# A fused attention and MLP layer: query blocks outermost, exponentials of 1536 columns, gelu once per block

## The chip, the cores and the metric

One core of one Trainium2 chip. All times are device microseconds (us) of one execution. The profile lists five engines: TensorE (PE; PEld is its weight load), ScalarE (ACT), VectorE (DVE), GpSimd (POOL) and SyncE (SP), which issues most of the DMAs on the pages here. The kernel before takes 1041.75 us (median of 3 runs, 1039.78 to 1043.16).

## The reference, cut to what matters

Sequence 2048, model width 512, 32 heads of 16, hidden width 1792, everything bf16:

```python
xn  = layernorm(x)
qkv = xn @ wqkv                               # 32 heads, Dh = 16
p   = softmax(q @ k.T * Dh ** -0.5)           # 32 x 2048 x 2048 exponentials
a   = (p @ v) @ wo
h   = gelu(layernorm(xn) @ w1 + b1)           # tanh form of gelu
out = x + a + h @ w2 + b2
```

The 134 million exponentials decide: in calls of 128 partitions (128x1024 before, mostly 128x1536 after) they are 1,048,576 columns, and both kernels compute all of them on ScalarE. Scores lie transposed (128 keys by 512 queries per head), so one *unit* of work is 512 columns; there are 2048 units.

## The kernel before

The outer loop goes over 8 sets of four heads, inside it over 4 query blocks of 512 and 16 key tiles. Per key tile: one *gang* of four small score matmuls, one for each head, on 32 rows of the array each (the four together last 0.40 us at 467.57, one such matmul 0.39 on average); two exponentials of two units; and one gang of four small p x v matmuls, which accumulate into one bank, o.

```python
psc = pctx.enter_context(tc.tile_pool(name="psc", bufs=3, space=PSUM))   # scores: three of two banks
...
for r in range(NR):                       # s, qt, kt
    emit_act(2 * r)                       # exp, 1024 columns
    if r + 1 < NR:
        emit_qk(r + 1)                    # 4 score matmuls
    if r >= 1:
        emit_pv(r - 1)                    # 4 p x v matmuls
    done = jobs.run(dense_per_round)      # up to 2.4 full matmuls of other work
    ...                                   # fills (zeros times ones) up to pe_fill = 3.0
    emit_act(2 * r + 1)
```

Three more places matter. The norms take square roots on ScalarE and go through all 16 token tiles before the first score. The MLP computes gelu from tanh, one call and four VectorE passes for each of 56 hidden tiles. Its results, and those of the output projection, are added to an f32 accumulator on VectorE:

```python
nc.scalar.activation(out=sd1[:], in_=mv[:, :, 1], func=AF.Sqrt, bias=eps_t[:], scale=1.0)
...
nc.vector.scalar_tensor_tensor(out=u[:, fi, :], in0=pre[:, fi, :], scalar=0.044715, ...)
nc.vector.scalar_tensor_tensor(out=u[:, fi, :], in0=u[:, fi, :], scalar=1.0, ...)
nc.scalar.activation(out=uv, in_=uv, func=AF.Tanh, scale=GELU_C)
nc.vector.scalar_tensor_tensor(out=ht[:, f0 + fi, :], in0=u[:, fi, :], scalar=1.0, ...)
...
groups = [[0, 1, 2], [3, 4, 5], list(range(6, NS - 1)), [NS - 1]]   # output projection, in pieces
```

Of the kernel before, what the change touches and what calls it, by code (L numbers as in the profile page):

```python
# [26 lines left out]
BOUND_INFL = 0.505  # L27
L_MIN = 1e-25
L_MAX = 1e6
GELU_C = float(np.sqrt(2.0 / np.pi))  # L30
_DBG = os.environ.get("PSM_DBG")


class _Jobs:

    NPRIO = 4

    def __init__(self, held):
        self.q = [[] for _ in range(self.NPRIO)]
        self.credit = 0.0  # L40
        self.held = held
        self.sticky = None
        self.activity = 0.0
        self.paused = set()

    def add(self, gen, prio):
        self.q[prio].append(gen)
        return gen

    def _first(self):  # L50
        if self.sticky is not None:
            return self.sticky
        for q in self.q:
            if q and q[0] not in self.paused:
                return q
        return None

    def step(self):
        q = self._first()
        if q is None:  # L60
            return None
        g = q[0]
        try:
            c = next(g)
        except StopIteration:
            q.pop(0)
            c = 0
            assert not self.held(), "job finished while holding the misc bank"
        self.sticky = q if self.held() else None
        if c == "pause":  # L70
            assert self.sticky is None
            self.paused.add(g)
            c = 0
        if isinstance(c, tuple):
            c, a = c
        else:
            a = c
        self.activity += a
        return c

    def run(self, budget):
        self.credit = min(self.credit, 0.0) + budget
        self.activity = 0.0
        self.paused = set()
        while self.credit > 0.0:
            c = self.step()
            if c is None:
                break
            self.credit -= c
        return self.activity  # L90

    def pending(self, gen):
        return any(gen in q for q in self.q)

    def finish(self, gen):
        while self.pending(gen):
            self.paused = set()
            self.step()

    def drain(self):  # L100
        while True:
            self.paused = set()
            if self.step() is None:
                break
        self.credit = 0.0
# [3 lines left out]
def kernel(  # L109
# [11 lines left out]
    dense_per_round: float = 2.4,  # L121
    pe_fill: float = 3.0,
# [13 lines left out]
    NKT = S // P  # L136
    TQ = QW // P
    assert S % QW == 0 and D % P == 0 and F % P == 0 and H % HS == 0
    SW = HS * DH
    NCH = QW // 32  # L140

    const = ctx.enter_context(tc.tile_pool(name="const", bufs=1))
    big = ctx.enter_context(tc.tile_pool(name="big", bufs=1))

    def gate_on(mm, gate):
        if gate is not None:
            tc.add_manual_dep(mm.ins, gate.ins.name, ORDER_DEP, reason="order gate")

# [3 lines left out]
    seln = const.tile([P, P], BF, name="seln")  # L152
    selr = const.tile([P, P], BF, name="selr")
    eps_t = const.tile([P, 1], F32, name="eps_t")
    onescol = const.tile([P, 1], F32, name="onescol")
    onescol2 = const.tile([P, 1], F32, name="onescol2")
    okmin = const.tile([P, 1], F32, name="okmin")
    ones_f = const.tile([P, 1], F32, name="ones_f")
    r2m1 = const.tile([P, NT], F32, name="r2m1")
    b1_sb = const.tile([P, FC], BF, name="b1_sb")  # L160
    b2_sb = const.tile([1, D], BF, name="b2_sb")
    flag_i = const.tile([1, 1], I32, name="flag_i")
    wq_pad = big.tile([P, JC, H, 32], BF, name="wq_pad")
    wk_pad = big.tile([P, JC, H, 32], BF, name="wk_pad")
    wv_sb = big.tile([P, JC, D], BF, name="wv_sb")
    wo_pad = big.tile([P, NS, D], BF, name="wo_pad")
    w1_sb = big.tile([P, JC, F], BF, name="w1_sb")
    w2_sb = big.tile([P, FC, D], BF, name="w2_sb")
    va_bufs = [big.tile([P, NKT, HS, 32], BF, name=f"va{i}") for i in range(2)]
    acc = big.tile([P, NT, D], F32, name="acc")  # L170
    kt0p = big.tile([P, S], BF, name="kt0p")
    kmx0 = const.tile([P, NQT], F32, name="kmx0")
    xnT_c = [big.tile([P, JC, QW], BF, name=f"xnT{tq}") for tq in range(NQT)]
    r2m1b = big.tile([P, S], BF, name="r2m1b")
# [3 lines left out]
    G = 4  # L178

    def load_acc(gate=None):  # L180
        for t0_ in range(0, NT, G):
            d_ = nc.gpsimd.dma_start(acc[:, t0_:t0_ + G, :], xv[:, t0_:t0_ + G, :])
            if gate is not None:
                tc.add_manual_dep(d_.ins, gate.ins.name, SYNC_DEP, reason="x first")

    with tc.tile_pool(name="start", bufs=1) as st, \
            tc.tile_pool(name="startw", bufs=3) as stw, \
            tc.tile_pool(name="pst", bufs=3, space=PSUM) as pst, \
            tc.tile_pool(name="psk", bufs=4, space=PSUM) as psk, \
            tc.tile_pool(name="psw", bufs=1, space=PSUM) as psw:  # L190
        x_sb = st.tile([P, NT, D], BF, name="x_sb")
        for gi_, t0_ in enumerate(range(0, NT, G)):
            (nc.sync if gi_ % 2 == 0 else nc.scalar).dma_start(
                x_sb[:, t0_:t0_ + G, :], xv[:, t0_:t0_ + G, :])
        with nc.allow_non_contiguous_dma(reason="tiny bias load"):
            nc.scalar.dma_start(b1_sb[:], B_b1.rearrange("(fc p) -> p fc", p=P))
        nc.scalar.dma_start(b2_sb[:], B_b2[None, :])

        make_identity(nc, ident_bf[:])
        nc.vector.memset(ones_bf[:], 1.0)  # L200
        nc.vector.memset(zeros_bf[:], 0.0)
        nc.vector.memset(ones_f[:], 1.0)
        nc.vector.memset(seln[:], 0.0)
        nc.vector.memset(selr[:], 0.0)
        for j in range(HS):
            nc.vector.memset(seln[32 * j:32 * j + DH, 32 * j + DH:32 * j + DH + 1], 1.0)
            nc.vector.memset(selr[32 * j:32 * j + 1, 32 * j + DH:32 * j + DH + 2], 1.0)
        nc.vector.memset(eps_t[:], LN_EPS)
        nc.vector.memset(okmin[:], 1.0)
        pm0 = psw.tile([P, 1], F32, tag="w", name="pm0")  # L210
        nc.tensor.matmul(pm0[:], lhsT=selr[:], rhs=ones_bf[:, 0:1], start=True, stop=True)
        nc.vector.tensor_copy(onescol2[:], pm0[:])
        for j in range(HS):
            nc.vector.memset(selr[32 * j:32 * j + 1, 32 * j + DH + 1:32 * j + DH + 2], 0.0)
        pm1 = psw.tile([P, 1], F32, tag="w", name="pm1")
        nc.tensor.matmul(pm1[:], lhsT=selr[:], rhs=ones_bf[:, 0:1], start=True, stop=True)
        nc.vector.tensor_copy(onescol[:], pm1[:])
        for jc in range(JC):
            nc.vector.memset(wk_pad[:, jc, :, DH:32], 0.0)
            nc.gpsimd.memset(wq_pad[:, jc, :, DH:32], 0.0)  # L220
        for va_i in va_bufs:
            nc.gpsimd.memset(va_i[:].rearrange("p k j r -> p (k j r)"), 0.0)
            nc.gpsimd.memset(va_i[:, :, :, DH:DH + 1], 1.0)

        stats = st.tile([P, NT, nc.vector.BN_STATS_DIM], F32, name="stats")
        mv = st.tile([P, NT, nc.vector.BN_AGGR_DIM], F32, name="mv")
        sd1 = st.tile([P, NT], F32, name="sd1")
        sd2 = st.tile([P, NT], F32, name="sd2")
        r1 = st.tile([P, NT], F32, name="r1")
        v2 = st.tile([P, NT], F32, name="v2")  # L230
        assert D <= nc.vector.BN_STATS_FMAX
        gate_stat = None
        for t in range(NT):
            nc.vector.bn_stats(out=stats[:, t, :], in_=x_sb[:, t, :])  # L234
            ag = nc.vector.bn_aggr(out=mv[:, t, :], in_=stats[:, t, :])
            if t == min(NT - 1, 2 * G):
                gate_stat = ag
        wqk = st.tile([P, JC, 2 * D], BF, name="wqk")
        wo_v = A_wo.rearrange("(s j r) c -> j r s c", j=HS, r=DH)
        loads = [(wqk[:, :, D:2 * D], wv_view[:, :, D:2 * D]),  # L240
                 (wqk[:, :, 0:D], wv_view[:, :, 0:D]),
                 (wv_sb[:], wv_view[:, :, 2 * D:3 * D]),
                 (w1_sb[:], B_w1.rearrange("(jc p) f -> p jc f", p=P)),
                 (w2_sb[:], B_w2.rearrange("(fc p) d -> p fc d", p=P))]
# [56 lines left out]
    def run_pass(slow):  # L301
# [43 lines left out]
        class _Ring:  # L345
# [5 lines left out]
            @staticmethod  # L351
            def first(mm):
                return mm
# [531 lines left out]
```

## Time and profile before

To compare the two kernels I use one account for both. For each exponential I take from the trace the time from its start to the start of the next one. Unhindered this is 0.903 us for 1024 columns in the kernel before and 1.330 for 1536 in the changed one. The 0.427 between them for 512 columns are 0.834 ns a column, which leaves 0.05 us a call; the sums below use columns x 0.8333 ns + 50 ns, which gives both. Their sum is the *floor*; what a step takes beyond it is other ScalarE work or a stall.

| kernel before, us of its profiled run (span 1038.8) | |
|---|---|
| first exponential starts | 40.2 |
| floor of 1024 exponentials | 925.0 |
| 56 tanh calls at 0.52 | 29.1 |
| stalls of ScalarE (rest of 60.4 beyond the floor) | 31.3 |
| from the last exponential's end to the span's end | 12.9 |

(The prediction used 0.91 for a step, so it has 932 for this floor and 25 for these stalls.) Next, the view of waits, with its columns: who waited, for whom; us in total, how often, longest.

```profile
ACT p L751 <- PE sc L741: 13.2, 31, 2.2
```

Exponentials waited visibly for score matmuls only 31 times, never over 2.2 us. The kernel before is close to its floor everywhere but at the start.

### The profile page before, as it was taken

How to read it: one execution, taken by the hardware profiler on the slowest of the kernel's cores; microseconds unless marked ns; L12 is line 12 of the kernel's file. 1: busy time of each engine (PE TensorE's matmuls, PEld its weight loads, DVE VectorE, ACT ScalarE, POOL GpSimd, SP SyncE). 2: the span in 40 equal slices, each digit the busy share in tenths (PEclk: the TensorE clock that was granted, in tenths of full speed). 3: DMA queues.
4: the chain of work that ended last, by engine and by line, in shares of the span. 5: the costliest groups of instructions: out<-in, count | busy, mean ns of one | idle time of the engine just before them, and what ended most of it. 6: DMA issues, size and time to landing. Idle time of an engine off the chain costs nothing.

```text
span 1038.8 us, 15620 instructions
## 1 busy us (share of the span) xinstructions
PE 835.0 (80%) x6085; PEld 251.2 (24%) x6197; DVE 452.5 (44%) x976; ACT 988.0 (95%) x1106; POOL 13.2 (1%) x19
## 2 busy tenths in 40 slices
PE   5778877888778889888778887788888877788885
PEld 2312221222212222222222222122222222222221
DVE  8543894513954413536924259451134432112222
ACT  2799999999999999999999999999999999999995
POOL 5000000000000000000000000000000000000000
PEclk8999999999989999999999999999999999999998
DMA  8800000000000000000000000000000000000000
GB/s 256 210 1 1 2 1 1 1 1 1 1 1 1 2 1 1 1 2 1 1 1 1 2 1 1 1 2 1 1 2 1 1 1 1 1 1 21 21 22 23
DMA packets 12913, 15.22 MB, mean 15 GB/s; under 512 B 2337, under 2 KB 10274, under 8 KB 12834
## 3 DMA queue, kind: packets, MB, share of 16 engines
q1 hardware_dynamic: 6704, 7.87, 2.9%
q0 software_dynamic: 2112, 4.19, 1.2%
q10 hardware_dynamic: 4018, 2.10, 0.7%
q8 instruction: 50, 0.82, 0.3%
q14 instruction: 29, 0.24, 0.1%
HBM read 9.97 MB, written 2.10 MB: 12 GB/s over the span
## 4 chain that ended last, share of the span: by engine, by line
ACT 56%; PE 22%; issue 13%; DVE 7%; DMA 1%; ACTq 0%; SPq 0%; DVEq 0%
ACT p L751 53%; PE sc L741 8%; PE o L768 4%; PE o L804 2%; ACT u L598 2%; PE pk L367 1%; PE pq L406 1%; PE po L626 1%; PE ph L580 1%; PE po L607 1%; DVE stats L234 1%; DVE pre L588 1%; DVE qraw L414 1%; PE pvp L476 1%; DMA x_sb<-in_A_x_dram 0%
## 5 line engine op out<-in xcount | busy, mean ns | idle before, releaser
L751 ACT ACTIVATE p<-sc 128x1024 bf16<-128x1024 f32 x1024 | 958.1, 1138 | 14.6 <-PE sc L741 13.2
L768 PE MATMUL o<-p,va 128*32 128x512 bf16 x2048 | 241.1, 391 | 45.7 <-ACT p L751 43.2
L741 PE MATMUL sc<-qt,kt 32*128 32x512 bf16 x1792 | 195.6, 386 | 95.1 <-ACT p L751 87.2
L804 PE MATMUL o<-ones_bf,zeros_bf 128*128 128x512 bf16 x514 | 165.4, 383 | 3.6 <-issue 3.0
L741 PEld LDWEIGHTS <-kt 32*128 32x128 bf16 x1792 | 49.2, 91 | 289.7 <-ACT p L751 265.8
L768 PEld LDWEIGHTS <-va 128*32 128x32 bf16 x2048 | 61.0, 93 | 225.5 <-ACT p L751 116.5
L506 DVE STREAM_TRANSPOSE ta<-o 128x512 f32<-128x512 f32 x32 | 22.9, 716 | 152.8 <-PE o L768 152.8
L580 PE MATMUL ph<-yT,w_sb 128*128 128x512 bf16 x210 | 63.5, 381 | 6.9 <-DVE pre L588 4.8
L632 DVE TENSOR_TENSOR acc<-po,acc 128x512 f32<-128x512 f32 x48 | 33.2, 691 | 77.7 <-PE po L626 69.5
L607 PE MATMUL po<-w_sb,ht 128*128 128x512 bf16 x210 | 63.0, 383 | 3.0 <-issue 1.8
L804 PEld LDWEIGHTS <-zeros_bf 128*128 128x128 bf16 x569 | 45.1, 97 | 72.0 <-issue 54.3
L616 DVE SCALAR_TENSOR_TENSOR acc<-po,acc 128x512 f32<-128x512 f32 x16 | 11.0, 689 | 112.8 <-PE po L613 112.8
L588 DVE TENSOR_SCALAR pre<-ph,b_sb 128x512 f32<-128x512 f32 x56 | 41.8, 747 | 11.8 <-PE ph L580 10.2
L600 DVE SCALAR_TENSOR_TENSOR ht<-u,pre 128x512 bf16<-128x512 f32 x56 | 38.5, 688 | 17.0 <-ACT u L598 16.4
L626 PE MATMUL po<-wo_pad,ont 128*128 128x512 bf16 x118 | 38.1, 389 | 6.6 <-DVE okr L533 2.7
L414 DVE TENSOR_SCALAR qraw<-pq,khalf 128x512 bf16<-128x512 f32 x31 | 23.1, 747 | 46.1 <-PE pq L406 46.1
L598 ACT ACTIVATE u<-u 128x512 f32<-128x512 f32 x56 | 42.5, 760 | 0.0
L374 DVE TENSOR_SCALAR kt<-pk,onescol 128x512 bf16<-128x512 f32 x28 | 20.8, 745 | 43.4 <-PE pk L367 43.4
L367 PE MATMUL pk<-xnT,wk_pad 128*128 128x512 bf16 x104 | 35.6, 403 | 4.7 <-DVE kmx L387 3.5
L592 DVE SCALAR_TENSOR_TENSOR u<-pre 128x512 f32<-128x512 f32 x56 | 38.4, 685 | 1.0
L595 DVE SCALAR_TENSOR_TENSOR u<-u,pre 128x512 f32<-128x512 f32 x56 | 38.4, 685 | 0.9
L406 PE MATMUL pq<-xnT,wq_pad 128*128 128x512 bf16 x115 | 34.7, 382 | 3.1 <-DVE qt L424 1.0
(107 smaller groups left out, 460.0 us busy)
## 6 DMA issues: line engine op xcount, KB each, us to landing
acc<-in_A_x_dram POOLq DMA_DIRECT2D x4, 1024.0 KB, 16.3
w_sb<-in_B_w_dram SPq DMA_DIRECT2D x2, 1792.0 KB, 19.5
x_sb<-in_A_x_dram ACTq DMA_DIRECT2D x2, 512.0 KB, 6.9
x_sb<-in_A_x_dram SPq DMA_DIRECT2D x2, 512.0 KB, 6.3
wqk<-in_A_wqkv_dram SPq DMA_DIRECT2D x2, 512.0 KB, 4.2
out_dram<-ot SPq DMA_DIRECT2D x8, 128.0 KB, 1.7
out_dram<-ot ACTq DMA_DIRECT2D x8, 128.0 KB, 1.7
wv_sb<-in_A_wqkv_dram SPq DMA_DIRECT2D x1, 512.0 KB, 6.2
```

What stands on the lines that cost most here:

```text
L367: mm = nc.tensor.matmul(pk[:], lhsT=wk_s[jc], rhs=xnT_c[tq][:, jc, :], start=(jc == 0), stop=(jc == JC - 1))
L406: mm = nc.tensor.matmul(pq[:], lhsT=wq_s[jc], rhs=xnT_c[tq][:, jc, :], start=(jc == 0), stop=(jc == JC - 1))
L580: mm = nc.tensor.matmul(ph[:], lhsT=w1_sb[:, jc, fc * P:(fc + 1) * P], rhs=yT[:, jc, :], start=(jc == 0), stop=(jc == JC - 1))
L588: _Chained.done(nc.vector.tensor_scalar(out=pre[:, fi, :], in0=ph[:], scalar1=b1_sb[:, fc:fc + 1], scalar2=None, op0=ALU.add))
L598: nc.scalar.activation(out=uv, in_=uv, func=AF.Tanh, scale=GELU_C)
L600: nc.vector.scalar_tensor_tensor(out=ht[:, f0 + fi, :], in0=u[:, fi, :], scalar=1.0, in1=pre[:, fi, :], op0=ALU.add, op1=ALU.mult)
L607: mm = nc.tensor.matmul(po[:], lhsT=ht[:, fc, c * P:(c + 1) * P], rhs=w2_sb[:, fc, :], start=(fc == 0), stop=False)
L626: mm = nc.tensor.matmul(po[:], lhsT=ont_tiles[s][:, qs], rhs=wo_pad[:, s, :], start=(i == 0), stop=(i == n - 1))
L741: mm = nc.tensor.matmul(sct[2 * r + j // 2][:, j % 2, :], lhsT=kt_t[lo:lo + 32, kt * P:(kt + 1) * P], rhs=qt_t[lo:lo + 32, qt * QW:(qt + 1 ...
L751: acts[k] = nc.scalar.activation(p_t[:].rearrange("p a b -> p (a b)"), sct[k][:].rearrange("p a b -> p (a b)"), AF.Exp, scale=float(DH) ** ...
L768: mm = nc.tensor.matmul(o_ps[lo:lo + 32, :], lhsT=va_t[:, kt, j, :], rhs=p_t[:, j % 2, :], start=(kt == 0), stop=(kt == NKT - 1), tile_pos ...
L804: nc.tensor.matmul(o_ps[:, :], lhsT=zeros_bf[:, :], rhs=ones_bf[:, :], start=False, stop=False, skip_group_check=True)
```

## The change

The intent is to start the exponentials after four token tiles instead of sixteen, to save the fixed cost (the 0.05 us above) of a third of the calls by making them 1536 columns long, and to take load off VectorE. Query blocks go outermost (4 blocks of 8 sets), so a block's MLP and output projection come together, in one PSUM accumulation, at its end. Eight PSUM banks are in use: two score buffers of three, one for o, and one spare through which all other matmul work passes. The order of all instructions comes from a small scheduler inside the kernel, a *plan*, which simulates the engines with a duration for each piece. The core of the diff, which replaces nearly all of the kernel:

```diff
-        psc = pctx.enter_context(tc.tile_pool(name="psc", bufs=3, space=PSUM))
+    TILES = ((0, 3), (3, 3))          # score buffers: banks 0-2 and 3-5
+    OB, MB = 6, 7                     # o, and the one spare bank
+    NPU = 18                          # p: 18 units
+    PEN = {1: 0.22, 2: 0.23, 3: 0.25, 4: 0.285}       # the plan's time of a gang
+    def mmd(n, cols=QW):                              # ... of n full matmuls
+        return n * (cols / 2400.0 + 0.0025)
...
-        nc.scalar.activation(out=sd1[:], in_=mv[:, :, 1], func=AF.Sqrt, ...)
+    def rsqrt(y, w, a):
+        ...                           # start value by integer operations
+        for _ in range(3):
+            I(nc.vector.scalar_tensor_tensor(out=a, in0=y, scalar=-0.5, in1=y, ...))
+            I(nc.vector.tensor_tensor(out=a, in0=a, in1=w, op=ALU.mult))
+            I(nc.vector.scalar_tensor_tensor(out=y, in0=a, scalar=1.5, in1=y, ...))
+        b = add("DVE", 1.0, frs, ...)                 # all twelve operations: 1.0 us in the plan
...
+        m = add("PE", mmd(4), fv, (xt_op[t], ld_wv,   # V projection of token tile t
+                kt_op[0, min(t // TQ + 1, NQT - 1)], q0), pr, ...)
...
-                nc.scalar.activation(out=uv, in_=uv, func=AF.Tanh, scale=GELU_C)
+            for h0 in (0, half):                      # once per block: 2 x 3584 columns
+                hv = ht[:, h0:h0 + half, :].rearrange("p a b -> p (a b)")
+                I(nc.scalar.activation(out=hv, in_=hv, func=AF.Gelu_apprx_tanh, scale=1.0))
...
+            for f0 in range(0, FC, 3):                # x + second MLP matmul, pieces of 3
+                m = add("PE", mmd(len(fcs)), part(fcs, f0 == 0, False), ...)
+            def fin(key=key, cs=cs, gs=gs):           # b2 + output projection: 9 in one piece
+                for n_, g in enumerate(gs):
+                    I(nc.tensor.matmul(ps[:, bk, :], lhsT=ont[:, g % NON, cs], ...))
```

The sums of p travel to memory and back as a reciprocal by four DMAs per set of heads, in place of two transposes on VectorE; the large GpSimd memsets are gone.

> **What bounds the kernel now.** I read the page first (busy shares, slices, groups), then ScalarE's timeline at the start, then the timeline of all engines in a steady stretch, then the timeline of the end.
>
> ```profile
> PE 835.0 (80%) x6085; PEld 251.2 (24%) x6197; DVE 452.5 (44%) x976; ACT 988.0 (95%) x1106; POOL 13.2 (1%) x19
> ACT  2799999999999999999999999999999999999995
> ...
> ACT 56%; PE 22%; issue 13%; DVE 7%; DMA 1%; ACTq 0%; SPq 0%; DVEq 0%
> ...
> L751 ACT ACTIVATE p<-sc 128x1024 bf16<-128x1024 f32 x1024 | 958.1, 1138 | 14.6 <-PE sc L741 13.2
> ...
> L598 ACT ACTIVATE u<-u 128x512 f32<-128x512 f32 x56 | 42.5, 760 | 0.0
> ```
>
> ScalarE (ACT) is busy 95%, its digits are 9 from the third slice to the last but one, and the chain that ended last is mostly its exponentials. TensorE's 80% contains 165.4 us of fill matmuls (the group that writes o from zeros_bf), so it has room on average. The only long time in which ACT is not at work on exponentials is the beginning:
>
> ```profile
> 30.87 0.69 ACT L284 ACTIVATE kt0p<-pk,onescol 128x512 bf16<-128x512 f32 x1
> 31.46 1.06 ACT L267 COPY xnT<-tpx 128x512 bf16<-128x512 bf16 x2
> 33.63 0.69 ACT L284 ACTIVATE kt0p<-pk,onescol 128x512 bf16<-128x512 f32 x1 [1.11 <-PE pk L282]
> 37.30 0.69 ACT L669 ACTIVATE qraw<-pq,nkh 128x512 bf16<-128x512 f32 x1 [2.98 <-PE pq L666]
> 40.20 1.94 ACT L751 ACTIVATE p<-sc 128x1024 bf16<-128x1024 f32 x2 [2.21 <-PE sc L741]
> ```
>
> The first exponential starts at 40.2 us. The last one ends at 1025.8 (it is in a row of seven that starts at 1019.26 and takes 6.71), the span ends at 1038.8: 13 us of tail. Now a steady stretch:
>
> ```profile
> 465.55 11.14 ACT L751 ACTIVATE p<-sc 128x1024 bf16<-128x1024 f32 x12
> ...
> 467.57 0.40 PE L741 MATMUL sc<-qt,kt 32*128 32x512 bf16 x4 [0.35 <-ACT p L751]
> ...
> 467.89 0.40 PE L768 MATMUL o<-p,va 128*32 128x512 bf16 x4
> ...
> 468.23 0.82 PE L626 MATMUL po<-wo_pad,ont 128*128 128x512 bf16 x3
> ...
> 469.40 0.40 PE L741 MATMUL sc<-qt,kt 32*128 32x512 bf16 x4 [0.35 <-ACT p L751]
> ```
>
> Twelve exponentials in 11.14 us, the last one 1.14 long: (11.14 - 1.14)/11 = 0.91 us from start to start. 1024 columns at 0.833 ns are 0.853, so one instruction costs 0.057 besides its columns. On TensorE a gang of four score matmuls holds the engine 0.32 us (467.57 to 467.89), a gang of four p x v matmuls 0.34 (to 468.23), and three full matmuls take 0.82 of which the last is 0.39 long, so they follow at (0.82 - 0.39)/2 = 0.215. A gang behind full matmuls starts about 0.31 after the last of them, so each switch costs about 0.1.
>
> The account of before: 1024 x 0.91 = 932; a tanh takes 0.52 to the next start (502.18 to 502.70 in the timeline), 56 x 0.52 = 29; together 961. The stretch 40.2 to 1025.8 is 985.6, so 25 us are stalls. 40.2 + 961 + 25 + 13 = 1039 of span, and the median of the runs is 3 above it.
>
> [...] The trace has the load at 1.28; at its second one the sqrt ends at 19.86 and the next activation starts at 21.17, 1.31 in all[...]. [...] here the mean granted clock is 0.986[...]. [...] the output stores here land after a median of 1.7.
>
> **The change, part by part.**
>
> The start. Only four token tiles have to be normed before the first scores, against sixteen. VectorE first does its memsets (about 4.5 us, from sizes and the 0.27 of a 128x256 memset), to about 5.3; tokens land no later (5.75 now, with bigger pieces). Statistics 4 x 0.83 = 3.3, to 8.6; twelve tiny Newton operations at 0.12 to 0.17, 1.7, to 10.3; four normings at 0.43, to 12; transposes and evacuation about 1.5, to 13.5; first Q and K projection on a clock that may be still half, 8 x 0.43 = 3.4, with three more statistics between on VectorE; evacuation 0.75, scores 0.5. I put the first exponential at 18: 22 us saved.
>
> ScalarE's floor. 2048 units of 512 columns are cut into 664 calls of 1536 and 28 of 1024 (the first 56 tiles alternate 3 and 2 units, then always 3). 664 x (1.280 + 0.057) = 888, 28 x 0.91 = 25.5: 913 against 932. Gelu: per block two calls of 3584 columns, 2.99 + 0.09 each, 8 of them 24.6; eight table loads at 1.3 to 1.6 with the lost overlap, 12 [...]. So 913 + 37 = 950 against 961. That is the smaller gain of the two; calls got fewer, but the tanh has been exchanged for gelu with table switches. Six copies of transposed tokens on ACT fall in the early phase, which TensorE bounds anyway. The five VectorE passes per hidden tile become one (56 x 4 x about 0.69 = 154 us off VectorE), which is off the path.
>
> Stalls of ScalarE, the term that decides. There are now two score buffers of three banks, not three of two: scores i+2 can start only when exponential i has ended and must be ready when i+1 ends. By the latencies in the trace (0.06 from the end of an exponential to the gang, 0.49 from the gang to the next exponential, where it was waited for) only about 0.7 us of other TensorE work fit between without a stall. I counted the compiled instruction order of the changed kernel between consecutive score gangs with the costs above (gang 0.325 and 0.331, full matmul 0.216, 0.1 per switch), ACT at 1.34 per full tile:
> - tiles 0 to 23: 100 full matmuls, 48 transposes, 18 p x v gangs, 41 us of TensorE against 27 of ACT. Excess 14.
> - tiles 186 to 215, 356 to 385, 526 to 565 (second MLP matmul and output projection just after a block ends, 40 to 48 full matmuls in ten tiles): excess 7.3, 7.4 and 5.8, together 20. Runs of nine (1.9 us) stand between two gangs, so this is a low estimate.
> - the last 16 tiles hold the same for the last block: 3 to 5.
> - everywhere else TensorE has 10 to 11.5 us for each 13.4 of ACT: no stall, about two fills per tile.
> Handoffs of the o bank, waits of the in-order TensorE for the four-DMA chain of the sums [...] and VectorE in the first set (12 statistics, 3 Newton runs, 25 evacuations, nearly 50 us): 4 more. Sum about 42, against 25 now: 17 given back.
>
> The tail keeps its shape (transpose, four projections, four adds, flag): 13.
>
> Sum: 18 + 950 + 42 + 13 = 1023 of span, plus 3 for the usual distance to the timed runs, plus 2 for what that count misses: 1028 us, 1.3% faster.
>
> **Rivals.** A: TensorE keeps up, ACT runs at its floor. For it: TensorE's average load is below ACT's, and the fill stretches are 20% free. Then 18 + 950 + 13 + 3 and some 10 of stalls, about 995. Against it: the count of the order, which is fixed when the kernel is built. B: the two-deep scores make every long TensorE run a stall; summing each tile's excess over 0.7 us of slack gives some 50 in place of 42, and blocked DVE or DMA waits come on top: 1040 to 1045, no gain at all. The kernel before speaks for it: the same count gives under 10 us of stalls there, where 25 are seen. C: the granted clock falls, since fills are now about 1.5 full matmuls per us (3 in 1.83 us before); but gangs are denser, 0.43 us of each us against 0.35, so I expect 0.97 or more[...]. D: the guard for the sums (now 64 and up, no shift of the exponent) fails and the general path runs[...]; scores here have a spread near 1.3, sums are thousands, so I give it 1%.
>
> **Range and chances.** The start is good to 1.5 us, the floor to 5 [...], the stalls to 15. Two per cent faster is 1021; it needs stalls below about 35. The count speaks against that, the fact that a rewritten schedule is seldom kept unless it pays speaks for it. 1005 to 1046 holds it 8 times in 10. Faster 0.34, within 2% 0.62, slower 0.04.
>
> **What would show it.** First exponential near 18 us; ACT's exponentials 692, of 1.33 to 1.34 from start to start where nothing is waited for; table loads 9, of 1.28; idle time of ACT before the exponentials released by the score matmuls, in the first 60 us and in three bursts of about 15 tiles after each block, 5 to 8 us each, and none in the fill stretches; TensorE near 1.0 clock. Wrong would be: ACT's digits 9 throughout (rival A), a first set over 55 us (VectorE, not TensorE), TensorE idle in the bursts waiting for the product of o and reciprocals (the DMA chain is too slow), or idle before exponentials spread over the fill stretches.

Passages are cut from the recorded prediction where marked. No term of its sum is among them: 18 + 950 + 42 + 13 came to 1023 of span, and with 3 and 2 to 1028 us. Of the figures it uses, the 0.833 ns a column had not been measured before the change; the traces of both kernels give the 0.834 above. The 0.216 of a full matmul is the commonest step from one to the next in both traces at full clock (0.216), and the gangs last 0.32 and 0.33 before (465.74 to 466.06 to 466.39). The half clock that it allows for at the start is in the trace of the kernel before, 0.5 from 15.5 to 25.8 us. That an engine takes its work in order, which it and two expectations use, shows in the changed kernel: its first copy of V starts on VectorE at 31.73, behind the last of twelve Newton operations (31.65), though the four matmuls that it needs, begun at 29.34, should end near 30.4 (an estimate: 3 x 0.216 + 0.39). That the clock follows the fills (rival C) was the author's guess; of the runs, e2 below comes nearest to it (124 matmuls in a stretch at 0.50, where the changed kernel has 172 at 1.00). "The load" is ACT_TABLE_LOAD, of 1.28 us.

## The result, and the profile after

The changed kernel takes **1055.95 us** (median of 4 runs, 1054.59 to 1056.20), against 1040.76 of the kernel before in the same rounds. A ratio here is the mean time of one kernel's fast runs over that of the other's of the same rounds, and the numbers on record come out when the profiled run is left out, so it is not quite the ratio of the medians: 1.0144, interval 1.0126 to 1.0161. All runs of this case were in the fast state. So it is 1.4% slower, where 1.3% faster was predicted, and outside the range.

The page after: busy time, the digits of the span in 40 slices, and three of the groups (busy us, mean ns | idle before, releaser).

```profile
PE 858.6 (82%) x5861; PEld 284.7 (27%) x5969; DVE 200.5 (19%) x417; ACT 967.7 (92%) x718; POOL 30.2 (3%) x131
...
ACT  4589999999988999999998999999998899999993
...
PEclk9999999997999999998999999998999999999799
...
L861 ACT ACTIVATE p_sb<-ps 128x1536 bf16<-128x1536 f32 (+1 forms) x692 | 927.0, 1617 | 53.7 <-PE ps L842 39.4
...
L1098 PE MATMUL ps<-wo_pad,ont 128*128 128x512 bf16 x119 | 28.8, 380 | 0.4 <-issue 0.3
...
L1056 ACT ACTIVATE ht<-ht 128x3584 bf16<-128x3584 bf16 x8 | 25.1, 3181 | 0.0
```

ScalarE's busy time fell by 20 us (988.0 to 967.7), as the longer calls promised, and the span grew by 13.6: ScalarE now waits. Its digits begin with 4, 5, 8 instead of 2, 7, 9 (an earlier start, but waits just after it), there are groups of 8 in three more places, and 3 at the end instead of 5. The exponentials idle 53.7 us before they start where before it was 14.6. The view of waits says for whom (L842 is the score matmul, L884 is p x v):

```profile
ACT p_sb L861 <- PE ps L842: 39.4, 48, 2.8
ACT p_sb L861 <- PE ps L884: 12.4, 5, 5.2
```

The account, with that of the best experiment (the last one below) for later:

| us | before | after | e11 |
|---|---|---|---|
| first exponential starts | 40.2 | 17.8 | 17.2 |
| floor of the exponentials | 925.0 | 908.4 | 908.4 |
| other ScalarE work | 29.1 (tanh) | 40.3 (gelu stops 37.5, six copies 2.8) | 28.1 (28 tanh calls, copies) |
| stalls | 31.3 | 69.3 | 24.9 |
| tail | 12.9 | 16.5 | 12.8 |
| span | 1038.8 | 1052.4 | 992.1 |

(The columns sum to a little under the span, because the last exponential's record, 1.44 us, is longer than its floor of 1.330.) The stalls of 69.3 lie as follows: 24.2 in the first 140 us; 7.9 in the 20 to 40 us after the gelu stops; 29.5 in three bursts just after a block ends (11.0, 8.9, 9.6); 4.0 in the last block's; 3.7 elsewhere.

**A gelu stop.** ScalarE's timeline (start, us, engine, line, operation, count, then the idle time before it), and after it TensorE's two first lines and one exponential of the time that follows:

```profile
232.34 1.28 ACT L1056 ACT_TABLE_LOAD   x1
233.64 6.27 ACT L1056 ACTIVATE ht<-ht 128x3584 bf16<-128x3584 bf16 x2
239.92 1.28 ACT L861 ACT_TABLE_LOAD   x1
241.22 4.13 ACT L861 ACTIVATE p_sb<-ps 128x1536 bf16<-128x1536 f32 x3
...
242.72 0.61 PE L842 MATMUL ps<-qz,kt 32*128 32x512 bf16 x3 [9.13 <-ACT p_sb L861]
...
243.81 1.89 PE L1180 MATMUL ps<-ones_bf,zeros_bf 128*128 128x512 bf16 x4
...
246.34 1.45 ACT L861 ACTIVATE p_sb<-ps 128x1536 bf16<-128x1536 f32 x1 [0.99 <-PE ps L842]
```

No exponential runs for 8.9 us; each stop costs 9.3 to 9.4 beyond the floor. Two table loads of 1.28 us stand in it, each within 0.02 us of the end of what ran before. TensorE idles 9.13 us, because both score buffers are full. When it returns a score gang takes 0.61 instead of 0.39 and four full matmuls 1.89 instead of 1.04: the clock records give 0.5 from 237.5 for 10.2 us, and the same after each of the four stops (10.2, 10.2, 10.2, 13.7 us; after the first one 3.4 us twice more, at 258.0 and 288.7). In that time ScalarE waits for scores.

**A burst.** The timeline just after the first block has ended (L1098 is the output projection; one matmul record of eight is missing from the trace):

```profile
304.53 1.45 ACT L861 ACTIVATE p_sb<-ps 128x1536 bf16<-128x1536 f32 x1 [0.39 <-PE ps L842]
...
304.69 0.39 PE L1095 MATMUL ps<-b_sb,ones_bf 1*128 1x512 bf16 x1
...
305.00 1.90 PE L1098 MATMUL ps<-wo_pad,ont 128*128 128x512 bf16 x7
...
306.84 0.60 PE L842 MATMUL ps<-qz,kt 32*128 32x512 bf16 x6
...
307.34 6.82 ACT L861 ACTIVATE p_sb<-ps 128x1536 bf16<-128x1536 f32 x5 [1.35 <-PE ps L842]
```

From 304.69 to 306.84 TensorE does nine full matmuls in a row, while the exponential that ran at 304.53 was over at 305.98. The next one waits 1.35 us for its scores. The six score matmuls at 306.84 are two gangs at once: both score buffers stood empty. This repeats for each of the block's four output tiles. Two other causes can be struck out here. The clock records give 1.0 while these runs hold up the scores (292.1 to 476.4, 486.7 to 725.6 and 735.8 to 971.4 us, which hold the three bursts). And TensorE does not wait for the four-DMA chain of the sums: its output projections (L1098 on the page above) have 0.4 us of idle time before them in the whole run, none of it put down to their input.

**The start.** VectorE, TensorE and ScalarE between 29 and 34 us:

```profile
29.34 1.90 PE L781 MATMUL ps<-wkv,xnT 128*128 128x512 bf16 x8
29.45 1.45 ACT L861 ACTIVATE p_sb<-ps 128x1536 bf16<-128x1536 f32 x1 [2.83 <-PE ps L842]
29.48 0.16 DVE L623 TENSOR_SCALAR lnv<-mv 128x4 f32<-128x4 f32 x1
...
31.73 0.68 DVE L788 CAST va<-ps 128x512 bf16<-128x512 f32 x1
...
33.42 0.40 PE L884 MATMUL ps<-p_sb,va 128*32 128x512 bf16 x4
...
33.91 1.02 ACT L861 ACTIVATE p_sb<-ps 128x1024 bf16<-128x1024 f32 x1 [3.02 <-PE ps L884]
```

The exponential at 33.91 waits 3.02 us for a p x v: the seven before it have filled the 18 units of p. That first p x v needs V, whose projection (L781) begins only at 29.34, since the plan lets V of the first token group wait for K of the second; and its evacuation (L788) stands on VectorE behind twelve Newton operations, 29.48 to 31.81 (0.20 from one start to the next).

**The tail.** The last p x v is at 1036.82. Then the last output tile's whole second MLP matmul still has to run, because it had to wait for the spare bank:

```profile
1036.82 0.40 PE L884 MATMUL ps<-p_sb,va 128*32 128x512 bf16 x4
...
1041.17 3.18 PE L1080 MATMUL ps<-w_sb,ht 128*128 128x512 bf16 x14
...
1044.60 1.47 PE L1098 MATMUL ps<-wo_pad,ont 128*128 128x512 bf16 x6
...
1047.12 0.69 DVE L1129 TENSOR_TENSOR ot<-ps,wkv 128x512 bf16<-128x512 f32 x1
```

### The profile page after: what moved, and what is told of

Same layout as the page of the kernel before. It is cut to its first block, busy times and chain, and to the rows that moved or that the text cites. A ratio compares the mean times of both kernels' runs of the same rounds, so it can differ in the third digit from the quotient of the medians.

```text
span 1052.4 us, 14247 instructions
## 1 busy us (share of the span) xinstructions
PE 858.6 (82%) x5861; PEld 284.7 (27%) x5969; DVE 200.5 (19%) x417; ACT 967.7 (92%) x718; POOL 30.2 (3%) x131
## 4 chain that ended last, share of the span: by engine, by line
ACT 48%; PE 24%; issue 19%; DVE 7%; DMA 1%; another core or an unknown queue 0%; ACTq 0%; DVEq 0%
ACT p_sb L861 45%; PE ps L842 5%; PE ps L1080 5%; PE ps L1042 4%; PE ps L884 4%; PE ps L1098 2%; PE ps L1180 2%; DVE ht L1047 1%; ACT ht L1056 1%; PE ps L781 1%; DVE stats L617 1%; DVE kt L717 1%; PE ps L701 1%; DVE xn_r L634 1%; ACT L861 0%
## 5 line engine op out<-in xcount | busy, mean ns | idle before, releaser
L861 ACT ACTIVATE p_sb<-ps 128x1536 bf16<-128x1536 f32 (+1 forms) x692 | 927.0, 1617 | 53.7 <-PE ps L842 39.4
L842 PE MATMUL ps<-qz,kt 32*128 32x512 bf16 x2048 | 270.4, 386 | 152.5 <-ACT p_sb L861 142.4
L1180 PE MATMUL ps<-ones_bf,zeros_bf 128*128 128x512 bf16 x911 | 264.0, 391 | 11.0 <-issue 10.8
L884 PE MATMUL ps<-p_sb,va 128*32 128x512 bf16 x2048 | 205.7, 394 | 0.0
L842 PEld LDWEIGHTS <-kt 32*128 32x128 bf16 x2048 | 87.0, 91 | 394.5 <-issue 384.1
L1180 PEld LDWEIGHTS <-zeros_bf 128*128 128x128 bf16 x986 | 71.7, 98 | 122.4 <-issue 86.1
L884 PEld LDWEIGHTS <-va 128*32 128x32 bf16 x2048 | 52.2, 93 | 121.7 <-issue 121.4
L1042 PE MATMUL ps<-yT,w_sb 128*128 128x512 bf16 x213 | 56.8, 379 | 5.0 <-DVE ht L1047 3.4
L1080 PE MATMUL ps<-w_sb,ht 128*128 128x512 bf16 x215 | 55.2, 381 | 0.8 <-issue 0.5
L1047 DVE TENSOR_SCALAR ht<-ps,b_sb 128x512 bf16<-128x512 f32 x56 | 42.0, 751 | 60.3 <-PE ps L1042 58.6
L1098 PE MATMUL ps<-wo_pad,ont 128*128 128x512 bf16 x119 | 28.8, 380 | 0.4 <-issue 0.3
L1080 PEld LDWEIGHTS <-ht 128*128 128x128 bf16 x224 | 19.0, 98 | 24.2 <-issue 8.2
L781 PE MATMUL ps<-wkv,xnT 128*128 128x512 bf16 x62 | 16.1, 381 | 1.7 <-DVE va L788 1.1
```

Source lines behind the costliest of these rows:

```text
L781: I(nc.tensor.matmul(ps[:, bk, :], lhsT=xnT[:, t // TQ, jc, (t % TQ) * P:(t % TQ + 1) * P], rhs=wv_sb[:, jc, :], start=(jc == 0), stop=(jc ...
L842: I(nc.tensor.matmul(ps[:, b0 + x, :], lhsT=kt[lo:lo + 32, s // 2, k * P:(k + 1) * P], rhs=qz[lo:lo + 32, qt % 2, s // 2, s % 2, :], start ...
L861: I(nc.scalar.activation(p_sb[:, s0:s1, :].rearrange("p a b -> p (a b)"), ps[:, b0:b0 + n, :].rearrange("p a b -> p (a b)"), AF.Exp, scale ...
L884: I(nc.tensor.matmul(ps[32 * j:32 * j + 32, OB, :], lhsT=va[:, k, h * VS:h * VS + 32], rhs=p_sb[:, unit_slot[u0 + j], :], start=(c == 0), ...
L1042: I(nc.tensor.matmul(ps[:, bk, :], lhsT=w1_sb[:, jc, fc * P:(fc + 1) * P], rhs=yT[:, jc, :], start=(jc == 0), stop=(jc == JC - 1)))
L1047: I(nc.vector.tensor_scalar(out=ht[:, fc, :], in0=ps[:, misc.bank(key), :], scalar1=b1_sb[:, fc:fc + 1], scalar2=None, op0=ALU.add))
```

## The experiments

**Theory** after these views: the stalls come from TensorE's time between two score gangs, which the plan counts too short. It has 0.25 for a score gang and 0.285 for p x v, where the trace has 0.32 and 0.33 (310.73 to 311.05 to 311.38), and nothing for the switch between gangs and full matmuls (about 0.1: a gang starts 0.31 to 0.32 after the last full matmul, where another full one starts after 0.216). So it places more than fits; the gelu stops and the tail add theirs. **Rivals:** the two-deep score buffers as such cost the time, whatever TensorE does; or the clock does, which falls after each stop. Three narrower theories for the first 140 us came later: **A**, VectorE's time bounds it; **B**, TensorE's; **C**, the order, V after the next group's K. (These letters are not those of the prediction's rivals.) The first four experiments ran together, then four, then three on another chip; the kernel before had medians of 1041.27, 1041.34 and 1040.80 us beside them.

**e1: no table switch.** The stop stays, with tanh, beside which exp needs no table load (the kernel before has two loads in all, none later than 19.88 us, with 56 tanh among its exponentials). It is the wrong function, on purpose, though the result still passed the comparison.

```diff
-                I(nc.scalar.activation(out=hv, in_=hv, func=AF.Gelu_apprx_tanh, scale=1.0))
+                I(nc.scalar.activation(out=hv, in_=hv, func=AF.Tanh, scale=1.0))
```

> The changed kernel with the gelu's function replaced by tanh, which shares its table set with the exponential (wrong result on purpose; the same elements are read and written, the same order of instructions, no table switch). Four gelu stops of the exponentials, 9.3 to 9.4 us each beyond a normal start-to-start time in the changed kernel, should shrink to about 6.1 each (2 x 2.99 plus overhead). Theory (table switches cost 1.3 us each plus the lost overlap, about 3.2 us per block): 12 to 14 us less, about 1043. Rival (the stop's aftermath, a halved clock after an idle TensorE, costs as much again): 15 to 20 us less.

Measured 1045.21 (1042.67 to 1046.23), ratio 1.0031 [1.0010, 1.0051]: 10.7 us less than the changed kernel, a little short of the 12 to 14. The stops shrank from 9.4 to 6.16, and no load stands in them any more:

```profile
232.99 6.56 ACT L1056 ACTIVATE ht<-ht 128x3584 bf16<-128x3584 bf16 x2
239.15 4.43 ACT L861 ACTIVATE p_sb<-ps 128x1536 bf16<-128x1536 f32 x3
244.57 1.45 ACT L861 ACTIVATE p_sb<-ps 128x1536 bf16<-128x1536 f32 x1 [0.99 <-PE ps L842]
```

In the profiled runs the four stops gave back 12.9 us and the stalls elsewhere took 3.9 again. So the table switches are about 13 of the 37.5 us (4 x 3.2), and the aftermath is not their doing: the clock still halves (6.8, 13.7, 6.8, 6.8 us), and the wait of 0.99 is there as it was. The whole run has one table load, at the start.

**e2: block-end work taken out.** The second MLP matmul and seven of the eight output projections of each output tile are removed; the result is wrong on purpose.

```diff
-                    for fc in fcs:
-                        I(nc.tensor.matmul(ps[:, bk, :], lhsT=ht[:, fc, cs], rhs=w2_sb[:, fc, :], ...))
...
-                for n_, g in enumerate(gs):
+                for n_, g in [(len(gs) - 1, gs[-1])]:
```

> The changed kernel with the second MLP matmul and seven of the eight output-projection matmuls taken away at each block's end (wrong result on purpose), everything else in the same order, the wait for the last set's sums kept. Theory (runs of full matmuls between two score gangs stall ScalarE, because only two score buffers exist): the bursts after each block (10, 9, 9 and 4 us) and 3 to 4 us of the tail go, 1018 to 1026. Rival (TensorE waits at a block's end for the four-DMA chain of the sums): bursts stay at over half, 1038 or more.

Measured 1040.17 (1038.08 to 1041.12), ratio 0.9986 [0.9966, 1.0006]. The theory was missed by 14 us, and the rival's numbers came true (1038 or more, bursts at over half): the three bursts fell only to 7.1, 4.7 and 5.6. Yet its mechanism is not seen: in this trace too TensorE is not listed as waiting for the product of o and the reciprocals, but for 1.4 us in the tail. The clock fell with the bursts (mean 0.918 against 0.974 in the profiled runs), so the run does not decide for the theory either. One stretch, with columns us, busy time of PE, PEld, DVE, ACT, POOL, then PEclk, DMA share and GB/s; first the changed kernel, then e2:

```profile
796.00:823.00 27.00, 26.65 (x172) 8.75 (x173) 3.62 (x6) 22.04 (x17) 0.72 (x3) 1.00 0.04 12
```

```profile
796.00:823.00 27.00, 24.45 (x124) 5.34 (x125) 5.15 (x8) 24.87 (x19) 0.95 (x4) 0.50 0.10 32
```

Without those matmuls the array ran all 27 us at half clock (0.50), so what was left took nearly as long as the whole had. Taking work away from TensorE is no clean test here.

**e3: the plan told the truth.** The work stays the same, and the result is right; only the order changes. Gangs cost what the trace shows, a run of full matmuls 0.1 more, such a run may start only if it ends at most 0.5 us after the next score gang could start, and the output projection is cut into pieces of three.

```diff
-    PEN = {1: 0.22, 2: 0.23, 3: 0.25, 4: 0.285}
+    PEN = {1: 0.32, 2: 0.32, 3: 0.325, 4: 0.33}
...
-        return n * (cols / 2400.0 + 0.0025)
+        return n * (cols / 2400.0 + 0.0025) + 0.1
...
+                if e == "PE":
+                    qk = [t for t, op in cand if op.fn.__name__ == "fqk"]
+                    if qk:
+                        cand = [(t, op) for t, op in cand
+                                if not op.dense or t + op.dur <= min(qk) + self.SLACK]
...
-                for n_, g in enumerate(gs):
+            for g0 in range(0, len(gs), 3):      # fin in pieces
```

> The changed kernel, correct, with a plan that is told the measured gang costs (0.325 and 0.33 in place of 0.25 and 0.285, 0.1 per run of full matmuls) and lets a run of full matmuls start only if it ends at most 0.5 us after the next score gang could start; the output projection is cut into three pieces. No work is removed. Theory: bursts after blocks shrink from 28 us to under 4, the early phase gives 3 to 8, the tail 2: 1012 to 1025. Rival (TensorE is short of time in all, so that delayed work comes back later as stalls): 1040 or more. Rival (early phase is VectorE's): early stalls stay at 20 us or more either way.

Measured 1029.59 (1027.75 to 1031.12), ratio 0.9893 [0.9870, 0.9915]: 26 us less than the changed kernel. Where that one has its burst, ScalarE now shows one row:

```profile
293.38 38.06 ACT L867 ACTIVATE p_sb<-ps 128x1536 bf16<-128x1536 f32 x28
```

Twenty-eight exponentials without a visible wait. The three bursts went from 11.0, 8.9 and 9.6 us to about 1 each, the last block's from 4.0 to nothing, with not one matmul of useful work less. That is the proof of the theory for the bursts; which of the three parts of the edit (gang times, rule, pieces of three) does how much of it was not taken apart. The run missed its range by 5, for two reasons: the first 140 us gave back under 3 of the 3 to 8 us expected (about 21.7 of stalls remain, as the rival on VectorE had said), and the tail grew from 16.5 to 21.2, since two whole accumulations of the last block now follow the last exponential.

**e4: three score buffers of two banks.** The rival of the depth: exponentials of 1024 columns as in the kernel before (18 of the early ones have 512).

```diff
-    TILES = ((0, 3), (3, 3))
+    TILES = ((0, 2), (2, 2), (4, 2))
```

> The changed kernel with three score buffers of two banks (1024-column exponentials, as before the change) in place of two of three banks. ScalarE's floor rises by about 325 more calls at 0.05, 17 us; TensorE gets 325 more score gangs at 0.325. Theory (TensorE's time between gangs is what stalls): bursts get longer, 1065 to 1090. Rival (the depth of two buffers is the whole cost): stalls outside gelu fall from 69 to about 30, 1030 to 1045.

Measured 1075.06 (1072.07 to 1084.26), ratio 1.0352 [1.0297, 1.0407]. The floor is 17 us higher (925.5), as it must be, and the time beyond the floor is 109.7 us, the same as in the changed kernel (109.6). So the theory's range was hit by the floor: the bursts did not get longer, as it had them, but are about 8 us each. A third buffer alone does not take them away. The run is not clean, though: its smaller exponentials need 1033 score gangs in place of 692, and a gang of two holds TensorE about as long as one of three (0.317 and 0.323 us in the changed kernel's trace, where p x v follows), so a gain by depth could be hidden behind that load. What makes the rival of the depth fall is e3, which has two buffers still and no bursts.

**e5: no Newton steps after the first group.** Three groups copy the first group's factors (wrong on purpose).

```diff
-            rsqrt(r1[:, sl], lnv[:, sl], lnv2[:, sl])
+            if g:
+                I(nc.vector.tensor_copy(r1[:, sl], r1[:, 0:4]))
+            else:
+                rsqrt(r1[:, sl], lnv[:, sl], lnv2[:, sl])
```

> The changed kernel with the Newton steps of the second to fourth token group taken away (one copy of the first group's factors in place of eleven small operations; slightly wrong result on purpose), the order of everything else kept. It takes about 3 x 2.1 us off VectorE in the first 45 us and nothing off TensorE. Theory A (the early stalls, 26 us beyond the floor in the first 56 exponentials, are VectorE's in-order queue, planned at 1.0 us per group where it takes 2.4): 6 to 10 us less, 1046 to 1050. Theory B (early stalls are TensorE's, 41 us of work against 27): under 3 us less, 1053 or more.

Measured 1052.86 (1052.24 to 1053.07), ratio 1.0111 [1.0094, 1.0128]: 3.1 us less, between the two theories and next to B's edge. The time beyond the floor from 20 to 60 us fell from 20.5 to 16.4. VectorE has a share in it, not the whole.

**e6: a quarter of the V projection.** One contraction of four (wrong on purpose), so TensorE has 48 full matmuls less at the start.

```diff
-            for jc in range(JC):
+            for jc in range(1):
```

> The changed kernel with the V projection cut to one of its four contractions (wrong result on purpose), order kept. It takes 48 full matmuls, 10.4 us, off TensorE in the first 60 us and nothing off VectorE. Theory B (TensorE bounds the early phase): 7 to 11 us less, 1045 to 1049. Theory A (VectorE): under 4 us less, 1052 or more. If both this and the run without Newton steps gain, the early phase is a chain through both in-order queues.

Measured 1056.85 (1054.66 to 1058.21), ratio 1.0144 [1.0123, 1.0164]: nothing gained. The run has the flaw of e2: its clock from 17 to 60 us was 0.80 (second fence) where the changed kernel's was 1.00 (first).

```profile
17.00:60.00 43.00, 35.72 (x224) 13.94 (x226) 38.01 (x118) 26.39 (x27) 0.00 (x0) 1.00 0.27 87
```

```profile
17.00:60.00 43.00, 34.30 (x186) 12.26 (x185) 37.00 (x117) 25.23 (x26) 0.00 (x0) 0.80 0.27 87
```

A's number (1052 or more) came true, but with the clock changed the run doesn't support A, nor refute B. What the first row does show: in the changed kernel TensorE is busy 35.7 of those 43 us and VectorE 38.0, ScalarE 26.4. The first two are busy for 83% and 88% of it.

**e7: e3 with VectorE's true times in the plan** (Newton run 2.4 us instead of 1.0, norming 0.36 instead of 0.22, evacuations 0.69 instead of 0.60; one of the lines is shown).

```diff
-        b = add("DVE", 1.0, frs, [st_op[t] for t in ts] + [mk_c], pr)
+        b = add("DVE", 2.4, frs, [st_op[t] for t in ts] + [mk_c], pr)
```

> The paced kernel with a plan that is also told the measured VectorE times (2.4 us for a group's Newton steps in place of 1.0, 0.36 for a norming, 0.68 for an evacuation). Same work. Theory A (the plan's order of the early phase is bad because its VectorE times are wrong): 4 to 10 us below the paced kernel's 1029.6, 1020 to 1026. Theory B (the early work itself does not fit): within 3 us of it.

Measured 1029.44 (1028.91 to 1029.76), ratio 0.9888 [0.9872, 0.9905]: no change from e3, as B had it. That the early work does not fit at all is not shown by this, though: e9 gains with another order of the same work.

**e8: e7 with gelu from tanh, on two hidden tiles at a time.** 28 calls of 1024 columns, no table switch, no stop; VectorE does the rest, as in the kernel before.

```diff
-                I(nc.scalar.activation(out=hv, in_=hv, func=AF.Gelu_apprx_tanh, scale=1.0))
+                hv = ht[:, fc - 1:fc + 1, :].rearrange("p a b -> p (a b)")
+                I(nc.scalar.activation(out=hv, in_=hv, func=AF.Tanh,
+                                       scale=2.0 * float(np.sqrt(2.0 / np.pi))))
```

> The paced kernel with true VectorE times, and the gelu computed as before the change, from tanh on two hidden tiles at a time with the rest on VectorE, so that no table is switched and ScalarE makes no stop. ScalarE: 28 tanh at about 0.95 are 27 us, in place of four stops of 9.4 us, 37.6, and of their aftermath at a half clock (1 to 3 us each). Theory (the one gelu per block costs more than it saves): 12 to 20 us below the run with true VectorE times. Rival (the extra VectorE passes, 120 us, hold up the evacuation of the scores' neighbours): no gain or slower.

Measured 1014.17 (1013.05 to 1014.42), ratio 0.9741 [0.9725, 0.9758]: 15.3 us less than e7, and the granted clock rose from 0.968 to 0.992. On ScalarE 37.5 us of stops became 25.3 us of calls (28 x 0.903), 12.2 less. Stalls fell by 4.7 (37.7 to 33.0 in the profiled runs: the aftermath is gone, a part came back elsewhere), and the tail grew by 1.4.

**e9: e8 with V first.** V of a token group waits for its own group's K only.

```diff
-        m = add("PE", mmd(4), fv, (xt_op[t], ld_wv, kt_op[0, min(t // TQ + 1, NQT - 1)], q0), pr, ...)
+        m = add("PE", mmd(4), fv, (xt_op[t], ld_wv, kt_op[0, t // TQ], q0), pr, ...)
```

> The paced kernel with tanh, and one dependency of the plan relaxed: a token tile's V projection may run once the keys of its own group are projected, not those of the next group. Theory C (in the first set the exponentials wait for a free p slot, so for the first p x v product, so for V, which the plan holds behind the next group's norms; the waits of exponentials for p x v are 13.9 us before 60 us in the run before this one): early stalls fall by 6 to 11, 1003 to 1008. Theory A (VectorE is simply full, 38 of 43 us busy): V first pushes the norms back, within 3 us of 1014.

Measured 1008.96 (1008.01 to 1014.32, 5 runs), ratio 0.9691 [0.9674, 0.9707]: 5.2 us less, and just short of what C expected. (e8 ran on the other chip; beside it the kernel before was 0.5 us slower.) The waits of the exponentials from 15 to 80 us, first in e8:

```profile
ACT p_sb L867 <- PE ps L890: 15.0, 6, 5.5
...
ACT p_sb L867 <- PE ps L848: 4.4, 2, 3.7
```

Then in e9, where no exponential waits for a p x v any more:

```profile
ACT p_sb L867 <- PE ps L848: 9.7, 5, 2.9
```

The waits for p x v (L890), 15.0 us, are gone altogether, and 5.3 of them came back in this stretch as waits for scores (L848). The profiled run is the slowest of the five, with 10.2 us at half clock from 78.5 on, so it is not read beyond this stretch. C is right on the first cause; behind it stands the next.

**e10: e9 with the last block's MLP done early.** Its second MLP matmul is accumulated before the block's attention is finished and kept in the f32 accumulator; the output projection is added to it.

```diff
-                pr = ts_(qt, NS - 1) + 8 + 4 * c
+                pr = ts_(qt, 4) + 4 * c
...
-                    out=acc[:, c, :], ps[:, misc.bank(key), :])), [m4], ...
+                    out=acc[:, c, :], in0=ps[:, misc.bank(key), :], in1=acc[:, c, :],
+                    op=ALU.add)), [m4, a0], ...
```

> The run before this one, with the last block's second MLP matmul moved ahead of its attention output (it no longer waits for the seventh set; its sum goes to the accumulator early, the seven sets are added later). Theory (the tail, 23 us from the last exponential's end to the end of the span in the run with tanh, is 13 plus whole accumulations of two output tiles that the single spare bank kept for the end): 8 to 10 us less. Rival (the tail is the flag and the stores): nothing.

Measured 998.74 (997.06 to 1000.29), ratio 0.9594 [0.9577, 0.9611]: 10.2 us less. The tail fell from 23.2 (22.9 in e8) to 12.3. After the last transposes only four matmuls and four adds remain, apart from the small operations of the flag:

```profile
985.06 0.72 DVE L975 STREAM_TRANSPOSE ta<-ps 128x512 f32<-128x512 f32 x1 [3.91 <-PE ps L890]
...
988.04 1.04 PE L1168 MATMUL ps<-wo_pad,ont 128*128 128x512 bf16 x4 [2.02 <-DVE ont L984]
...
988.53 2.48 DVE L1171 TENSOR_TENSOR ot<-ps,wkv 128x512 bf16<-128x512 f32 x4
```

**e11: e10 with two Newton steps instead of three.** The result still agrees with the reference.

```diff
-        for _ in range(3):
+        for _ in range(2):
```

> The run before this one, with two Newton steps for each norm in place of three (still far below bf16 rounding). Takes 0.6 us per token group off VectorE, 0.6 of it before the first exponential. Theory A: 1 to 3 us less. Theory C alone: 0.6 us less.

Measured **995.15** (993.44 to 996.21), ratio 0.9561 [0.9545, 0.9577]: 3.6 us less, more than either theory expected. The first exponential came 1.3 us earlier than in e10 (17.24 against 18.57), although three operations of 0.2 us are 0.6; but in the runs e1, e2, e5 and e6, which leave the start alone, it came anywhere from 17.5 to 18.5, so part of this can be scatter. The stalls are 4.0 us less in the profiled runs. This version beats both kernels: by 4.4% the one before, and by 5.7% the changed one (0.9561 / 1.0144 = 0.943; the two never ran in the same rounds).

## Why the prediction was wrong

- **The start: right, in part by luck.** 18 predicted, 17.80 measured. The Newton run took 2.4 us (8.32 to 10.70), not 1.7, and shorter terms made up for it: the memsets and statistics were over at 8.3, not 8.6, and the four normings took 1.38, not 1.7.
- **The floor and gelu: right.** 913 + 37 = 950 predicted. The floor is 908.4 (steps of 1.330, not 1.337) and the stops 37.5, together 945.9.
- **The term that failed: "Sum about 42".** The stalls are 69.3. That it *decides* was seen, and most of the places; the main parts were too small, and two were missing:
  - the first 24 tiles, 14 predicted: 18.4. And from there to 140 us, where the prediction has "no stall", 5.8 more. The count of TensorE's work saw no p x v that waits for V, which waits for K and for VectorE. That both have a part in it is shown by e9 (5.2 us) and e5 (3.1 us).
  - the bursts, 7.3 + 7.4 + 5.8 = 20: in the tiles that it names 8.0 + 8.4 + 9.1 = 25.5, and with the tiles around them 29.5. The count took each stretch as a whole, so a light tile could pay for a heavy one. A run of nine full matmuls between two gangs costs its tile over a microsecond (1.35 us of waiting at 307.34), which nothing gives back. The prediction's own text calls it a low estimate, and its rival B, which counts each tile over 0.7 us, got 50 for all stalls; that was nearer, and still too low, as was its 1040 to 1045.
  - the aftermath of a gelu stop: not in the prediction, 7.9 measured. It has "no stall" for everywhere else, and has gelu on ScalarE alone. That TensorE idles 9.13 us behind full score buffers and returns at a clock of 0.5 for 10.2 us was missed; the prediction asks only for the clock's mean.
  - the last block, 3 to 5 predicted: 4.0, right. Handoffs and VectorE in the first set, 4 predicted: 3.7 lies elsewhere in the run, but was not traced to these.
- **The tail: "keeps its shape", 13.** It is 16.5. The one spare bank keeps the last output tile's MLP sum waiting until the bank is free; e10 took this out.

Sum of the misses: 27.3 of stalls, 3.5 of tail, 2.8 of copies on ScalarE which the prediction had put under work that costs nothing, less 4.1 for the floor and 0.2 for the start: 29.3. The prediction had a span of 1023, measured was 1052.4. Its rival A (TensorE keeps up, 995) is what e11 reaches, but only with the order mended and the stops taken out. Its rival C (the clock's mean falls below 0.97) did not happen: 0.970 to 0.974. One count in it is wrong without consequence: gelu had four VectorE passes per hidden tile, not five, so VectorE lost 115 us by this (157.1 to 42.0), not 154, and off the path.

What stays open: how the 14 us still beyond the floor from 20 to 60 us in e11 (2.8 of them for the six copies) divide between TensorE and VectorE. e5 and e9 each took a part, and e6, meant to tell, was spoilt by its clock.

## What to carry to other kernels

A count of an engine's load over a stretch is no count of its stalls: between two pieces of work that the bounding engine waited for, only the buffers' slack was free here, and each longer run cost its excess at once (nine full matmuls from 304.69 to 306.84: a wait of 1.35). If an order is planned from durations, take the durations from a trace; this kernel went from 1.4% slower to 1.1% faster by that and a rule of pacing built on it (e3). And a long call on the bounding engine can cost more than its own time: here TensorE, which feeds it, fell idle behind each stop (9.13 us at the first) and came back at half clock (0.5 for 10.2 us), and the stalls in the 20 to 40 us after the four stops came to 7.9 us.
